# A two-layer attention and gMLP kernel: the spatial bias loaded once and whole, two weights loaded later, a P ring of 41 places and a new scheduler table

## The chip, the cores and the metric

The kernel runs on one core of one Trainium2 chip. The metric is device time in microseconds, the median of several runs. A core has TensorE (PE, matrix products into PSUM), VectorE (DVE), ScalarE (ACT, here the exponentials and GELUs), GpSimd (POOL) and SyncE (SP, which here issues every DMA). Each engine works through its own list of instructions in order; between engines semaphores say what is finished.

## The reference

Four blocks follow each other on an input of 2048 rows by 512, in bfloat16: attention, gated MLP, and both once more with the same weights. Each block normalises its input and adds its result to it.

```python
def _A_ref(x, wq, wk, wv, wo):
    H = 32; Dh = D // H                        # 32 heads of 16, one shared key and value head
    q = (x @ wq).reshape(B, S, H, Dh).transpose(0, 2, 1, 3)
    k = x @ wk
    v = x @ wv
    p = _softmax(einsum('bhqd,bkd->bhqk', q, k) * Dh ** (-0.5))
    o = einsum('bhqk,bkd->bhqd', p, v)
    return o.transpose(0, 2, 1, 3).reshape(B, S, H * Dh) @ wo

def _B_ref(x, w_in, w_sp, b_sp, w_out):
    z = _gelu(einsum('bsd,df->bsf', x, w_in))  # F = 1792, halves of 896
    z1 = z[..., :Fh]
    z2 = _layernorm(z[..., Fh:])
    g = einsum('ts,bsf->btf', w_sp, z2) + b_sp[None, :, None]
    return einsum('bsf,fd->bsd', z1 * g, w_out)

x = A_x
x = x + _A_ref(_layernorm(x), ...)
x = x + _B_ref(_layernorm(x), ...)
x = x + _A_ref(_layernorm(x), ...)
x = x + _B_ref(_layernorm(x), ...)
```

The product with `w_sp` is the spatial sum: it mixes all 2048 rows, and `b_sp` is its bias, one value for each of the 2048 output rows `t`.

## The kernel before

**A planner writes the program.** The kernel is Python that plans the whole execution before it emits it. Every piece of work is a `Task` with an engine, a cost and predecessors; `Sched` walks through planned time, and at every event each idle engine picks what is ready by priority (`step_act`, `step_dve`, `step_pool`, `step_pe`, `step_sp`). The order in which tasks are picked is the order of instructions on the engine; on the chip each waits for its semaphores, not for planned times. What the planner takes wrongly, for instance the landing of a DMA, becomes a wait on the chip, and everything behind it on that engine waits too. The preferences of the planner (how many scores DVE gets, how deep products with V go, when other work is let in) are class attributes of `Kernel`; the table `PLAN` sets other values for steps of 1250 ns of planned time (`follow`, `STEP`).

**Attention.** Rows are normalised tile by tile (16 tiles of 128 rows): `ln` writes `xn`, a DMA transposes it into `z1`'s space (lines 1634, `z<-xn`; the first two tiles go through PE, L1773), PE makes keys and values (L1871, L1874) and queries (L1901). A score matmul (L2468) covers 128 keys and 512 query columns of a head, into one of eight PSUM banks. Two engines turn scores into unnormalised probabilities P: ACT by an exponential, one bank at a time (L2665) or two (L2666), and DVE by an integer form (L2557) whose two further terms, the ramps, are made on POOL or DVE (L2561, L2577, one, two or four at a time). A block on ACT takes one place of the ring `Pb`, a block on DVE three. `NPS` is the number of places, of 1 KB in each partition; a place is free again when the product with V (L2725) has read it. `slot_ok` and `pick_exp` let an exponential or ramp be planned only when a place is free.

The queries come in chunks (`CHUNKS`). When a chunk is finished, `attn_out` copies the sums out (`oT`, L1959), transposes them by DMA into `oP`, divides (reciprocal L2105, product L2122 on POOL), transposes again (`onT`), multiplies by `wo` (L2065), adds to `X`, normalises and transposes into `xnT2`. The last chunk of a layer goes through PE instead of DMA.

**MLP.** `mlp_in` multiplies by `w_in` (L2161, L2222) and applies GELU on ACT in bursts between exponentials, ten in all, each with two loads of ACT's function table (L2968). `spatial` adds up the spatial sum in five passes over the source rows, in each layer; a pass takes the rows whose `z2` is ready, runs beside attention, and goes through four quarters of 512 output rows (`tc`). For each quarter `slab` loads the transposed part of `w_sp` into `wstr` (L1642, eight places of one tile, so two quarters), and for each of seven blocks `f` PE sums (L2280) and DVE adds the result to `gp` (L2290). In the first pass the addend is the bias, in later ones `gp` itself. The last pass (`last_pass`: L2319, L2321, DVE L2329, POOL L2340) gates with `z1` and multiplies by `w_out` (L2350).

**The bias.** `bspc` holds one quarter, 512 values, copied to all partitions. For every quarter of the first pass SP loads it anew, 128 KB as written, after the last addition of the previous quarter has read it (`bs_use`):

```python
if pi == 0:
    lb = self.dma(self.bspc[:], self.B_b_sp[tc * 512:(tc + 1) * 512].partition_broadcast(P), 131072,
                  self.bs_use, prio=2, tag="ldb", gate=lambda: self.s.t > self.WSP_FROM)
```

**Loads of weights.** `x`, `wk`, `wv` and `wq` are issued at the start. `wo` (512 KB), `w_in` (1792 KB) and `w_out` (896 KB) have a gate: they may be planned when planned time has passed `W_FROM` = 45000 ns. Loads for the spatial sum have the gate `WSP_FROM` = 75000 ns. All DMAs, transpositions included, go through SP's one queue. `dma_w` is the planner's cost of a `wstr` load on SP.

The functions that follow are those that the change touches and what calls them.

Of the kernel before, what the change touches and what calls it, by code (L numbers as in the profile page):

```python
# [6 lines left out]
BF16 = mybir.dt.bfloat16  # L7
# [63 lines left out]
def c_mm(n, cols):  # L71
# [5 lines left out]
    9: dict(FILL_MIN=3, PV_EFF=0.8, ACT_MAX=1, DVE_HIGH=1200),  # L77
    10: dict(PV_MAX=3, PV_LEAST=4),
    11: dict(ACT_LOW=700, FILL_BUSY=3, PV_LEAST=4, DVE_LEAD=-300),
    12: dict(ACT_LOW=1050, FILL_BUSY=3, PV_LEAST=4, DVE_LEAD=300),  # L80
    13: dict(ACT_LOW=1050, FILL_BUSY=3, PV_LEAST=4, DVE_LEAD=300, POOL_TOP=2500),
    15: dict(SLACK_HI=650, POOL_TOP=2500),
    16: dict(PV_LEAST=4),
    17: dict(PV_LEAST=4),
    18: dict(PV_LEAST=4, SHARE=0.45),
    19: dict(PV_MAX=4, DVE_LEAD=300, DVE_HIGH=1200, QUADP=0),
    20: dict(SLACK_HI=800, FILL_MIN=4, PV_MAX=4, DVE_LEAD=300, POOL_TOP=2500, QUADP=0),
    21: dict(SLACK=350, PV_EFF=0.8),
    22: dict(SLACK=350, PV_LEAST=4, PV_EFF=0.8),
    23: dict(SLACK=350, ACT_LOW=700, PV_LEAST=4, PV_EFF=0.8, COLS=0),  # L90
    24: dict(SLACK=350, ACT_LOW=1400, PV_LEAST=4, PV_EFF=0.8, COLS=0),
    25: dict(SLACK=200, DVE_LEAD=-300, POOL_TOP=2500, SCORE_CAP=5),
    26: dict(SLACK=200, DVE_LEAD=-300, POOL_TOP=3500, SCORE_CAP=5),
    27: dict(SLACK=200, DVE_LEAD=-300, POOL_TOP=3500, SCORE_CAP=5),
    28: dict(SLACK=200, DVE_LEAD=-300, POOL_TOP=3500, MISC_T=700, ACT_MAX=1, SCORE_CAP=5),
    29: dict(SLACK=200, DVE_LEAD=-300, MISC_T=700, ACT_MAX=1, SCORE_CAP=5),
    30: dict(SHARE=0.31, POOL_TOP=2500),
    31: dict(SHARE=0.45, POOL_TOP=2500, QUADP=0),
    32: dict(FILL_MIN=4, PV_EFF=0.8),
    33: dict(PV_LEAST=4, QUADP=0),  # L100
    34: dict(PV_LEAST=4, QUADP=0),
    35: dict(PV_LEAST=4, SHARE=0.4, MISC_T=2500, QUADP=0),
    36: dict(ACT_LOW=1700, PV_LEAST=4, PV_EFF=0.8, SHARE=0.4, MISC_T=2500, DVE_HIGH=2400, QUADP=0),
    37: dict(ACT_LOW=1700, PV_LEAST=4, PV_EFF=0.8, SHARE=0.4, POOL_TOP=2500, MISC_T=2500, DVE_HIGH=2400, QUADP=0),
    38: dict(ACT_LOW=1700, PV_LEAST=4, PV_EFF=0.8, SHARE=0.4, POOL_TOP=2500, MISC_T=2500, SCORE_CAP=5, DVE_HIGH=2400, QUADP=0),
    39: dict(ACT_LOW=1700, PV_LEAST=4, PV_EFF=0.8, SHARE=0.45, POOL_TOP=2500, MISC_T=2500, SCORE_CAP=5, DVE_HIGH=2400, QUADP=0, QUADD=0),
    40: dict(PV_LEAST=8, SHARE=0.31, SCORE_CAP=7, DVE_HIGH=1200),
    42: dict(PV_LEAST=4),
    43: dict(SLACK_HI=300, PV_EFF=0.8, MISC_T=700, DVE_HIGH=1200),
    44: dict(SLACK_HI=300, PV_EFF=0.8, MISC_T=700, DVE_HIGH=1200),  # L110
    45: dict(SLACK_HI=300, PV_EFF=0.8, MISC_T=700, DVE_HIGH=1200),
    46: dict(SLACK_HI=300, PV_EFF=0.8, POOL_TOP=2500, MISC_T=2500, DVE_HIGH=2400),
    47: dict(POOL_TOP=2500),
    48: dict(POOL_TOP=2500),
    49: dict(FILL_BUSY=3, DVE_LEAD=-300, HOLD=400),
    51: dict(FILL_BUSY=3, SHARE=0.28, POOL_TOP=3500, HOLD=400),
    52: dict(FILL_BUSY=3, SHARE=0.28, POOL_TOP=3500, HOLD=400, ACT_MAX=1),
    53: dict(POOL_TOP=7000),
    54: dict(POOL_TOP=7000),
    55: dict(SLACK=450, SLACK_HI=400, PV_LEAST=8, POOL_TOP=3500, SCORE_CAP=7),  # L120
    56: dict(SLACK=450, SLACK_HI=400, PV_LEAST=8, POOL_TOP=3500, SCORE_CAP=7),
    57: dict(SLACK=450, SLACK_HI=400, PV_LEAST=8, POOL_TOP=3500, SCORE_CAP=7),
    58: dict(SLACK=450, SLACK_HI=400, ACT_LOW=1400, PV_LEAST=8, POOL_TOP=3500, SCORE_CAP=7, QUADD=0),
    59: dict(SLACK=450, SLACK_HI=650, ACT_LOW=1400, PV_MAX=1, PV_LEAST=8, POOL_TOP=3500, SCORE_CAP=7, QUADD=0),
    60: dict(SLACK=450, SLACK_HI=650, ACT_LOW=1400, FILL_BUSY=3, PV_MAX=1, PV_LEAST=8, POOL_TOP=3500, SCORE_CAP=7, DVE_HIGH=1200, QUADD=0),
    61: dict(SLACK=450, SLACK_HI=650, ACT_LOW=1400, FILL_BUSY=3, PV_MAX=1, PV_LEAST=8, POOL_TOP=3500, SCORE_CAP=7, DVE_HIGH=1200, QUADD=0),
    63: dict(ACT_MAX=1),
    64: dict(ACT_LOW=900, PV_MAX=4, SHARE=0.28, HOLD=0, MISC_T=700),
    65: dict(MISC_T=2500, COLS=0),
    66: dict(COLS=0),  # L130
# [12 lines left out]
    81: dict(PV_MAX=4, DVE_LEAD=-600, POOL_TOP=7000, COLS=0),
    82: dict(PV_MAX=1),
    83: dict(FILL_MIN=3, POOL_TOP=2500, MISC_T=2500),
    84: dict(SLACK=350, ACT_LOW=1700, FILL_MIN=3, PV_MAX=3, MISC_T=2500, DVE_HIGH=1200),
    85: dict(ACT_LOW=1050, SHARE=0.36),
    86: dict(ACT_LOW=1050, PV_EFF=0.8, SHARE=0.36, HOLD=400),
    87: dict(SHARE=0.31),
    88: dict(FILL_BUSY=3, SHARE=0.28, DVE_LEAD=300, POOL_TOP=3500),  # L150
    89: dict(SHARE=0.36),
    90: dict(SHARE=0.36, POOL_TOP=2500),
    91: dict(SHARE=0.36, POOL_TOP=2500, MISC_T=2500),
    92: dict(FILL_BUSY=4, PV_MAX=4, SHARE=0.36, POOL_TOP=2500, MISC_T=2500),
    93: dict(FILL_BUSY=4, PV_MAX=4, SHARE=0.36, POOL_TOP=2500, MISC_T=2500),
    94: dict(FILL_BUSY=4, PV_MAX=4, SHARE=0.36, POOL_TOP=2500, MISC_T=2500),
    96: dict(FILL_MIN=3, SHARE=0.28, POOL_TOP=2500, MISC_T=2500),
    97: dict(SLACK=150, FILL_MIN=3, SHARE=0.28, POOL_TOP=2500, MISC_T=2500, SCORE_CAP=7),
    99: dict(SCORE_CAP=5),
    100: dict(PV_LEAST=4, SCORE_CAP=5),  # L160
    102: dict(POOL_TOP=2500),
    104: dict(PV_LEAST=4),
    105: dict(SHARE=0.4, HOLD=400),
    106: dict(ACT_LOW=1050, SHARE=0.4, POOL_TOP=2500, HOLD=400, DVE_HIGH=2400),
    107: dict(SLACK_HI=300, PV_MAX=4, PV_EFF=0.8),
    108: dict(SLACK_HI=300, PV_MAX=4, PV_EFF=0.8, POOL_TOP=2500),
    109: dict(SLACK_HI=300, PV_MAX=4, PV_EFF=0.8, POOL_TOP=2500, SCORE_CAP=5),
    110: dict(SLACK=600, SLACK_HI=650, FILL_MIN=3, SHARE=0.45),
    111: dict(SLACK=450, SLACK_HI=650, FILL_MIN=3, SHARE=0.45, QUADP=0),
    112: dict(SLACK=350, SLACK_HI=650, FILL_MIN=3, SHARE=0.45, COLS=3300, QUADP=0),  # L170
    113: dict(SLACK=350, SLACK_HI=650, FILL_MIN=3, SHARE=0.45, POOL_TOP=7000, COLS=3300, QUADP=0),
    114: dict(SLACK=350, SLACK_HI=650, FILL_MIN=3, PV_LEAST=4, SHARE=0.45, POOL_TOP=7000, COLS=3300, QUADP=0),
    115: dict(SLACK=350, SLACK_HI=650, FILL_MIN=3, PV_LEAST=4, SHARE=0.45, POOL_TOP=7000, COLS=3300, QUADP=0),
    116: dict(SLACK=350, SLACK_HI=650, ACT_LOW=1400, FILL_MIN=3, PV_LEAST=4, SHARE=0.45, POOL_TOP=7000, COLS=3300, DVE_HIGH=1200, QUADP=0),
    117: dict(SLACK_HI=800, FILL_MIN=3, POOL_TOP=3500, SCORE_CAP=7),
    118: dict(SLACK_HI=800, FILL_MIN=3, DVE_LEAD=300, POOL_TOP=3500, SCORE_CAP=7),
    119: dict(SLACK_HI=800, FILL_MIN=3, DVE_LEAD=300, POOL_TOP=3500, ACT_MAX=1, SCORE_CAP=7),
    121: dict(SLACK_HI=800, POOL_TOP=3500),
# [2990 lines left out]
```

## Time and profile before

| What | Before |
|---|---|
| median of three runs | 1503.27 us (1502.33 to 1505.92) |
| profiled execution, its own time | 1499.42 us |
| its span, first to last instruction | 1497.7 us |
| PE busy | 1433.2 us (96%) |
| DVE busy | 1383.0 us (92%) |
| ACT busy | 1377.4 us (92%) |
| POOL busy | 1037.3 us (69%) |
| mean granted clock of PE | 0.998 |
| bytes moved by DMA | 47.55 MB |
| exponentials of two banks, of one | 1212, 339 |

The profile is of one execution, and its times are from the first instruction. The page gives each engine's busy time; the chain of work that ended last, followed back from the end; and groups of equal instructions with their number, busy time, mean, and the idle time of the engine just before them with what ended it. A mean is from issue to end: where instructions overlap, their distance is shorter. The trace can be asked besides for waits by who waited for whom, for engines' busy time in stretches, and for the chain or the instructions in order of time. A line number names the line of the kernel that recorded the instruction.

In outline: the first attention layer runs from about 10 to 690 us, with GELU bursts and the first four passes of the spatial sum in it; the seam to the second layer takes until about 800, the second layer until 1435, and the rest is the tail.

### The profile page before, as it was taken

The numbers are of one execution on the slowest core, as the hardware profiler recorded it, in microseconds if no ns is written. First come the engines' busy times: TensorE is split into PE (matmuls) and PEld (weight loads), VectorE is DVE, ScalarE is ACT, GpSimd is POOL, SyncE is SP. The second block draws the span as 40 slices with busy tenths as digits, with TensorE's granted clock in tenths as the row PEclk, the third lists the DMA queues.
The fourth block names the chain that finished last, engine by engine and source line by source line (L and its number), as shares of the span: only waits on it lengthen the run. The fifth ranks groups of instructions, "written<-read, shape, count | busy, mean of one in ns | idle before, by whom it ended". The sixth has DMA issues, their size and how long they took to land.

```text
span 1497.7 us, 35502 instructions
## 1 busy us (share of the span) xinstructions
PE 1433.2 (96%) x14120; PEld 473.1 (32%) x14120; DVE 1383.0 (92%) x2605; ACT 1377.4 (92%) x1725; POOL 1037.3 (69%) x1152
## 2 busy tenths in 40 slices
PE   8999899999999999999999988999999999999999
PEld 3332232222322322233643322322223223222345
DVE  8899998999899999989767999899998999999886
ACT  7999999999999999996589999999999999999950
POOL 6677768878688688864114767677776786888737
PEclk9999999999999999999999999999999999999999
DMA  4420001112011111112121001001111111211111
GB/s 111 114 43 12 9 18 26 26 26 40 18 26 33 23 32 30 37 20 40 21 41 32 16 12 16 15 23 26 26 37 19 30 33 19 44 30 28 28 33 57
DMA packets 156627, 47.55 MB, mean 32 GB/s; under 512 B 148913, under 2 KB 155953, under 8 KB 156465
## 3 DMA queue, kind: packets, MB, share of 16 engines
q1 hardware_dynamic: 156464, 45.28, 15.2%
q8 instruction: 115, 1.88, 0.5%
q14 instruction: 48, 0.39, 0.1%
HBM read 6.98 MB, written 2.10 MB: 6 GB/s over the span
## 4 chain that ended last, share of the span: by engine, by line
ACT 53%; PE 36%; DVE 7%; DMA 2%; issue 0%; POOL 0%; SPq 0%; DVEq 0%
ACT Pb L2666 46%; PE ps_all L2725 9%; PE ps_all L2468 9%; PE ps_all L2280 7%; ACT Pb L2665 6%; DVE Pb L2557 4%; PE ps_all L2161 3%; PE ps_all L2350 3%; PE ps_all L2222 3%; PE ps_all L2321 1%; DMA bspc<-in_B_b_sp_dram 1%; DVE Pb L2577 1%; DMA z<-xn 1%; DVE gp L2290 1%; ACT L2968 1%
## 5 line engine op out<-in xcount | busy, mean ns | idle before, releaser
L2666 ACT ACTIVATE Pb<-ps_all 128x1024 bf16<-128x1024 f32 x1212 | 1154.3, 1138 | 12.8 <-PE ps_all L2468 11.9
L2577 POOL TENSOR_SCALAR Pb<-Pb 128x1024 int16<-128x1024 int16 (+1 forms) x732 | 803.4, 1097 | 212.0 <-DVE Pb L2577 163.4
L2557 DVE TENSOR_SCALAR Pb<-ps_all 128x512 int16<-128x512 f32 x1333 | 858.2, 684 | 39.7 <-PE ps_all L2468 33.6
L2468 PE MATMUL ps_all<-z,kT 32*128 32x512 bf16 x4096 | 535.8, 385 | 45.3 <-ACT Pb L2666 25.4
L2725 PE MATMUL ps_all<-Pb,V 128*32 128x512 bf16 x6762 | 531.9, 385 | 4.2 <-DVE Pb L2557 1.0
L2468 PEld LDWEIGHTS ps_all<-z,kT 32*128 32x128 bf16 x4096 | 136.2, 91 | 570.6 <-ACT Pb L2666 393.5
L2280 PE MATMUL ps_all<-wstr,z 128*128 128x512 bf16 x784 | 224.1, 384 | 1.8 <-DVE gp L2290 1.4
L2665 ACT ACTIVATE Pb<-ps_all 128x512 bf16<-128x512 f32 x339 | 205.8, 719 | 6.1 <-PE ps_all L2468 5.9
L2577 DVE TENSOR_SCALAR Pb<-Pb 128x1024 int16<-128x1024 int16 (+1 forms) x451 | 195.7, 471 | 0.4
L2725 PEld LDWEIGHTS ps_all<-Pb,V 128*32 128x32 bf16 x6762 | 124.6, 94 | 225.9 <-issue 119.5
L2290 DVE TENSOR_TENSOR gp<-ps_all,gp 128x512 f16<-128x512 f32 x168 | 113.2, 683 | 1.2 <-PE ps_all L2280 0.8
L2280 PEld LDWEIGHTS ps_all<-wstr,z 128*128 128x128 bf16 x784 | 51.5, 97 | 93.8 <-issue 41.7
L1724 POOL TENSOR_SCALAR ln_rs<-ln_mv 128x1 f32<-128x1 f32 (+2 forms) x52 | 11.6, 225 | 97.2 <-DVE ln_mv L1734 90.4
L2561 POOL TENSOR_SCALAR Pb<-Pb 128x512 int16<-128x512 int16 x79 | 48.8, 617 | 40.3 <-DVE Pb L2577 22.3
L2350 PE MATMUL ps_all<-w_out,z 128*128 128x512 bf16 x224 | 58.4, 380 | 0.3 <-DVE z L2329 0.2
L2122 POOL TENSOR_TENSOR o_norm<-oP,rdn 128x128 bf16<-128x128 bf16 (+1 forms) x84 | 39.7, 495 | 21.4 <-DVE Pb L2577 12.1
L2161 PE MATMUL ps_all<-w_in,xnT 128*128 128x448 bf16 x256 | 53.2, 353 | 0.9 <-ACT xnT L1785 0.7
L2222 PE MATMUL ps_all<-xnT,w_in 128*128 128x512 bf16 (+3 forms) x336 | 51.5, 308 | 0.0
L2174 DVE BATCH_NORM_STATS2 st<-z 128x6 f32<-128x448 bf16 x64 | 35.6, 604 | 13.8 <-ACT z L2166 13.6
L1959 DVE CAST oT<-ps_all 128x512 bf16<-128x512 f32 x64 | 43.9, 686 | 4.2 <-PE ps_all L2725 4.1
L1733 DVE BATCH_NORM_STATS2 ln_st<-X 128x6 f32<-128x512 bf16 x64 | 43.3, 682 | 1.7 <-DMA X<-in_A_x_dram 1.5
L2236 ACT ACTIVATE z<-ps_all 128x512 bf16<-128x512 f32 (+2 forms) x62 | 31.4, 562 | 13.7 <-PE ps_all L2222 13.6
(76 smaller groups left out, 768.4 us busy)
## 6 DMA issues: line engine op xcount, KB each, us to landing
out_dram<-X SPq DMA_DIRECT2D x16, 128.0 KB, 1.7
w_in<-in_B_w_in_dram SPq DMA_DIRECT2D x1, 1792.0 KB, 9.1
X<-in_A_x_dram SPq DMA_DIRECT2D x3, 512.0 KB, 7.8
bspc<-in_B_b_sp_dram SPq DMA_DIRECT2D x8, 128.0 KB, 3.7
oP<-oT SPq DMA_TRANSPOSE x60, 2.4
w_out<-in_B_w_out_dram SPq DMA_DIRECT2D x1, 896.0 KB, 7.2
wstr<-in_B_w_sp_dram SPq DMA_TRANSPOSE x40, 4.1
X<-in_A_x_dram SPq DMA_DIRECT2D x2, 256.0 KB, 3.2
```

The costliest lines, as they stand in the source:

```text
L2161: ins = e.matmul(self.ps32[:, b, 0:448], self.xnT2[:, buf, kd, o:o + P], self.w_in[:, kd, FH + h * 448:FH + (h + 1) * 448], start=(kd == 0 ...
L2222: ins = e.matmul(self.ps32[:, b, i * nq:(i + 1) * nq], self.w_in[:, kd, f * P:(f + 1) * P], self.xnT2[:, buf, kd, x0:x0 + nq], start=(kd = ...
L2280: ins = e.matmul(self.ps32[:, b, :], self.z2[:, (s0 + i) % Z2R, f * P:(f + 1) * P], self.wstr[:, sl[i // SLAB][1] + i % SLAB, :], start=(i ...
L2290: return Task("dve", c_ps(512), lambda e: e.tensor_tensor(self.gp[:, tc, f, :], self.ps32[:, bank(), :], src, ALU.add), dps, self.GP_P, ta ...
L2350: ins = e.matmul(self.ps32[:, b, :], self.z1[:, tc, f, o:o + P], self.w_out[:, f, :], start=(f == 0), stop=(f == NF - 1))
L2468: ins = e.matmul(self.ps32[:, jb[i].i, :], self.kT[32 * j:32 * j + 32, u.half, kt * P:(kt + 1) * P], q, tile_position=(32 * j, 0), start=T ...
L2557: return lambda e: e.tensor_scalar(self.Pi[:, dst(), :], self.ps32[:, bank, :], EBIAS + lo, lo, op0=ALU.add, op1=ALU.max)
L2561: return lambda e: e.tensor_scalar(self.Pi[:, dst(), :], self.Pi[:, src(), :], lo, 1.0, op0=ALU.add, op1=ALU.mult)
L2577: return lambda e: e.tensor_scalar(self.several(self.Pi, dst), self.several(self.Pi, src), lo, 1.0, op0=ALU.add, op1=ALU.mult)
L2665: return e.activation(self.Pb[:, ss[0], :], self.ps32[:, bs[0], :], ACTF.Exp, scale=ESCALE)
L2666: return e.activation(self.two(self.Pb, *ss), self.two(self.ps32, *bs), ACTF.Exp, scale=ESCALE)
L2725: ins = e.matmul(self.ps32[32 * j:32 * j + 32, u.bank.i, :], self.V[:, var, kt, :], self.Pb[:, sl.i, :], tile_position=(0, 32 * j), start= ...
```

## The change

- `bspc` grows from 512 to 2048 values in each partition, and one DMA (`ldbs`, 512 KB as written) fills it for both layers, with the gate `WSP_FROM`. The eight loads by quarter and `bs_use` go. The first pass reads its quarter out of it.
- `w_in` and `w_out` get the gate `WSP_FROM` (75000) instead of `W_FROM`. Their priorities put them behind the `wstr` loads and the bias. `wo` keeps `W_FROM`, which goes from 45000 to 48000.
- `NPS` goes from 44 to 41. Three places are 3 KB in each partition, as much as `bspc` grows.
- `dma_w` gives SP's cost of a `wstr` load by another formula: 2010 ns for four tiles (1859 before), 1410 for three (1645), 1230 for two (1430). It changes the plan only.
- `PLAN` is another table: 1071 steps have an entry instead of 1051, 952 have one in both, and none of these is the same. The order on every engine is therefore another. Line numbers rise by about 20 (L2665 and L2666 become 2686 and 2687, L2725 becomes 2746, L2290 becomes 2313).

```diff
 PLAN = {
-    9: dict(FILL_MIN=3, PV_EFF=0.8, ACT_MAX=1, DVE_HIGH=1200),
-    10: dict(PV_MAX=3, PV_LEAST=4),
...
 }
...
     WSP_FROM = 75000
-    W_FROM = 45000
-    NPS = 44
+    W_FROM = 48000
+    NPS = 41
...
-        self.bspc = self.sb([P, 512], BF16, "bspc")
+        self.bspc = self.sb([P, S], BF16, "bspc")
...
         def cost():
-            occ = 1000 + nbytes / 610.0
+            occ = 1230 + 600 * max(0.0, nbytes / 131072 - 2.7)
             self.wide_done = max(self.s.t + 3200, self.wide_done) + 500 + nbytes / 250.0
...
         self.ldo = self.dma(self.wo[:], ..., 524288, prio=2.5, gate=late)
-        self.ldin = self.dma(self.w_in[:], ..., 1835008, prio=2.5, gate=late)
-        self.ldout = self.dma(self.w_out[:], ..., 917504, prio=2.5, gate=late)
+        def later():
+            return s.t > self.WSP_FROM
+        self.ldin = self.dma(self.w_in[:], ..., 1835008, prio=2.5, tag="ldb", gate=later)
+        self.ldout = self.dma(self.w_out[:], ..., 917504, prio=2.6, tag="ldb", gate=later)
+        self.ldbs = self.dma(self.bspc[:], self.B_b_sp.partition_broadcast(P), 524288, prio=2.4, tag="ldb", gate=later)
...
                 if pi == 0:
-                    lb = self.dma(self.bspc[:], self.B_b_sp[tc * 512:(tc + 1) * 512].partition_broadcast(P), 131072,
-                                  self.bs_use, prio=2, tag="ldb", gate=lambda: self.s.t > self.WSP_FROM)
-                    self.bs_use = []
+                    lb = self.ldbs
...
-                        src = self.bspc[:] if pi == 0 else self.gp[:, tc, f, :]
+                        src = self.bspc[:, tc * 512:(tc + 1) * 512] if pi == 0 else self.gp[:, tc, f, :]
...
-                    if pi == 0:
-                        self.bs_use.append(outs[0])
...
-        self.bs_use = []
```

More of the change, by code (lines that the diff above doesn't have):

```diff
@@ L87 @@
[L87 to L94, printed above, removed]
@@ new lines @@
+    67: dict(FILL_BUSY=3, PV_MAX=3, PV_LEAST=8),
+    68: dict(PV_MAX=1, HOLD=0),
+    69: dict(HOLD=400),
+    70: dict(SLACK_HI=800, COLS=0),
+    71: dict(SLACK_HI=800, POOL_TOP=3500, COLS=0),
+    72: dict(SLACK=350, SCORE_CAP=5),
+    73: dict(SLACK=350, FILL_BUSY=3, POOL_TOP=7000, HOLD=400, SCORE_CAP=5, QUADD=0),
+    74: dict(COLS=0),
+    75: dict(PV_MAX=1, QUADD=0),
+    77: dict(ACT_LOW=700),
+    78: dict(ACT_LOW=700),
+    79: dict(ACT_LOW=700),
+    80: dict(ACT_LOW=1050, FILL_MIN=3, PV_MAX=1, HOLD=400, MISC_T=700, QUADP=0),
@@ new lines @@
+    350: dict(FILL_BUSY=3, PV_MAX=1, PV_LEAST=8, HOLD=400, COLS=3300),
+    351: dict(POOL_TOP=7000, MISC_T=700),
+    352: dict(POOL_TOP=7000, MISC_T=700),
+    354: dict(POOL_TOP=2500),
+    355: dict(PV_MAX=1),
+    356: dict(PV_MAX=1),
+    357: dict(SHARE=0.28, POOL_TOP=2500),
+    358: dict(SLACK=450, ACT_LOW=500),
+    359: dict(ACT_MAX=1),
+    360: dict(FILL_BUSY=3, COLS=0),
+    361: dict(SLACK_HI=800, PV_MAX=1, POOL_TOP=7000, SCORE_CAP=5, DVE_HIGH=2400),
+    362: dict(SHARE=0.31, DVE_HIGH=1200),
@@ new lines @@
+    553: dict(SLACK=600, HOLD=400, COLS=3300, DVE_HIGH=2400),
+    554: dict(SLACK=600, HOLD=400, COLS=3300, DVE_HIGH=2400),
+    555: dict(ACT_LOW=1050, SCORE_CAP=7),
+    556: dict(SHARE=0.36),
+    557: dict(DVE_LEAD=300),
+    558: dict(FILL_MIN=3, DVE_LEAD=300),
+    562: dict(QUADD=0),
+    563: dict(ACT_MAX=1, QUADP=0),
+    564: dict(ACT_MAX=1, QUADP=0),
+    565: dict(ACT_MAX=1, QUADP=0),
+    566: dict(ACT_MAX=1, QUADP=0),
+    567: dict(ACT_MAX=1, QUADP=0),
+    568: dict(ACT_MAX=1),
@@ new lines @@
+    736: dict(SLACK=450, HOLD=0),
+    737: dict(SLACK=450, HOLD=0),
+    739: dict(PV_LEAST=4, DVE_LEAD=300, MISC_T=700),
+    740: dict(PV_LEAST=4, DVE_LEAD=300, HOLD=400, MISC_T=700),
+    741: dict(FILL_MIN=4),
+    742: dict(POOL_TOP=2500),
+    743: dict(PV_MAX=1),
+    744: dict(ACT_LOW=900, MISC_T=2500, COLS=2900),
+    745: dict(DVE_HIGH=1200),
+    746: dict(ACT_LOW=900, SCORE_CAP=7),
+    747: dict(COLS=0),
+    748: dict(COLS=0),
+    749: dict(PV_EFF=0.8),
+    750: dict(PV_EFF=0.8, SHARE=0.45, DVE_LEAD=-300),
@@ new lines @@
+    815: dict(PV_LEAST=8, SHARE=0.36, MISC_T=700, DVE_HIGH=1200),
+    816: dict(SLACK_HI=400, FILL_BUSY=3, SHARE=0.24),
+    817: dict(SLACK_HI=400, FILL_BUSY=3, PV_MAX=1, SHARE=0.24),
+    818: dict(POOL_TOP=2500),
+    819: dict(POOL_TOP=2500),
+    820: dict(PV_EFF=0.8, HOLD=400),
+    821: dict(SLACK=600, PV_MAX=1, POOL_TOP=7000, MISC_T=700, QUADP=0),
+    822: dict(HOLD=400, QUADP=0),
+    824: dict(PV_MAX=1),
+    825: dict(PV_MAX=4),
+    826: dict(PV_MAX=4, PV_EFF=0.8, COLS=3300),
+    827: dict(FILL_MIN=4, PV_MAX=4),
@@ L1128 @@
+    1181: dict(SLACK=200, SLACK_HI=400, FILL_MIN=4, PV_MAX=1, SHARE=0.28, DVE_LEAD=300, QUADP=0, QUADD=0),
+    1184: dict(SLACK=600, FILL_BUSY=3, PV_LEAST=4),
+    1185: dict(SLACK=600, FILL_BUSY=3, PV_LEAST=4),
+    1186: dict(SLACK=600, FILL_BUSY=3, PV_LEAST=4),
+    1189: dict(SLACK=450, SLACK_HI=400, QUADP=0),
+    1190: dict(SLACK=450, SLACK_HI=400, QUADP=0),
 }
@@ L1816, in setup @@
         self.ldo = self.dma(self.wo[:], self.A_wo.rearrange("(c p) n -> p c n", p=P), 524288, prio=2.5, gate=late)
-        self.ldin = self.dma(self.w_in[:], self.B_w_in.rearrange("(kd p) f -> p kd f", p=P), 1835008, prio=2.5, gate=late)
-        self.ldout = self.dma(self.w_out[:], self.B_w_out.rearrange("(c p) n -> p c n", p=P), 917504, prio=2.5, gate=late)
+        def later():
+            return s.t > self.WSP_FROM
+        self.ldin = self.dma(self.w_in[:], self.B_w_in.rearrange("(kd p) f -> p kd f", p=P), 1835008, prio=2.5, tag="ldb", gate=later)
+        self.ldout = self.dma(self.w_out[:], self.B_w_out.rearrange("(c p) n -> p c n", p=P), 917504, prio=2.6, tag="ldb", gate=later)
+        self.ldbs = self.dma(self.bspc[:], self.B_b_sp.partition_broadcast(P), 524288, prio=2.4, tag="ldb", gate=later)
         self.ldv = ldv
```

2042 lines of the change are left out of this document (1001 added, 1041 removed).

## The prediction

> **What bounds the kernel now.** I read the page first: its engine shares, the clock row, the chain and the costliest groups.
>
> ```profile
> PE 1433.2 (96%) x14120; PEld 473.1 (32%) x14120; DVE 1383.0 (92%) x2605; ACT 1377.4 (92%) x1725; POOL 1037.3 (69%) x1152
> ...
> ACT 53%; PE 36%; DVE 7%; DMA 2%; issue 0%; POOL 0%; SPq 0%; DVEq 0%
> ...
> L2666 ACT ACTIVATE Pb<-ps_all 128x1024 bf16<-128x1024 f32 x1212 | 1154.3, 1138 | 12.8 <-PE ps_all L2468 11.9
> ...
> L2665 ACT ACTIVATE Pb<-ps_all 128x512 bf16<-128x512 f32 x339 | 205.8, 719 | 6.1 <-PE ps_all L2468 5.9
> ```
>
> ACT's exponentials (L2665, L2666) carry half of the chain. They idle only 12.8 + 6.1 = 18.9 us before them, nearly all for a score matmul (L2468). Outside the seam between the layers and the tail, ACT is full: whoever delays a score matmul by more than the scores in stock moves the end. So I looked for that idle time, in a table of stretches (columns: stretch; length, then busy us of PE, PEld, DVE, ACT, POOL; clock; DMA share; GB/s):
>
> ```profile
> 256.00:264.00 8.00, 6.76 (x73) 1.67 (x70) 6.54 (x12) 6.95 (x9) 5.03 (x6) 1.00 0.60 85
> 320.00:324.00 4.00, 3.02 (x36) 0.68 (x28) 3.35 (x6) 3.50 (x5) 3.68 (x5) 1.00 0.02 7
> 1000.00:1008.00 8.00, 6.50 (x46) 1.35 (x42) 5.87 (x10) 5.71 (x7) 5.11 (x5) 0.79 0.02 5
> 1060.00:1064.00 4.00, 2.52 (x21) 0.56 (x21) 2.74 (x5) 2.75 (x4) 2.47 (x4) 1.00 0.06 15
> 50.00:54.00 4.00, 1.92 (x24) 0.71 (x21) 1.97 (x6) 2.21 (x4) 2.09 (x2) 1.00 1.21 226
> 54.00:60.00 6.00, 5.86 (x56) 1.21 (x56) 4.31 (x10) 4.88 (x6) 2.23 (x4) 0.72 0.08 25
> ```
>
> In the first four ACT lacks 1.05 + 0.50 + 2.29 + 1.25 = 5.1 us, in the last two 1.79 + 1.12 = 2.9. The waits and the chain in order of time name the causes:
>
> ```profile
> DVE gp L2290 <- DMA bspc<-in_B_b_sp_dram: 5.6, 4, 1.8
> ```
> ```profile
> 46.61 5.77 DMA z<-xn
> 52.38 0.14 issue
> 52.52 0.38 PE ps_all L1871 x4
> ```
> ```profile
> w_in<-in_B_w_in_dram SPq DMA_DIRECT2D x1, 1792.0 KB, 9.1
> ```
>
> Four times the addition to `gp` stands at the head of DVE for the next quarter of the bias; the scores that DVE turns into P (L2557) queue behind it, their PSUM banks stay taken, PE can issue no scores, ACT dries up. Four other quarters of the bias cost ACT nothing. At 46.61 the last transposition of `xn` takes 5.77 us (median of its group 2.5) because `w_in`, issued at 42.75, takes 9.1 us to land; PE waits 1.93 us for it at L1871.
>
> **Part by part, in us of the profiled execution** (span 1497.7, own time 1499.42; the median of the runs, 1503.27, lies 3.85 above and I let that stand).
>
> *Bias whole.* Eight SP issues of 0.58 us and 128 KB become one of 512 KB, at about 77. First use is the first pass of the spatial sum at 229: 150 us of cover. L2290 then never waits for the bias: -5.1. Next late could be `wstr` of the same quarter, but it is asked for two quarters ahead (issued at 254.99, needed from about 285, median 4.1 to land), and the first pass otherwise waits only for PE, 0.3 in all now. Bounds: 0 if another wait stands in the same place, -5.1; I take -5.1, since the DMA is named as ender of all four.
>
> *w_in, w_out later.* In the instruction lists of the new program all 14 transpositions of `xn` are issued before `wo`, and `w_in`, `w_out` come behind two `wstr` loads, at about 78. The last transposition should take 2.5, no wait: -2.9. `wo` (4.7 to land) goes out about 48, first read at 77.9. What is delayed instead: 3.2 MB at the 400 GB/s of the stretch from 46 to 50 are 8 us, behind two `wstr` loads, so the queue is free at some 88 to 90. The next SP entries in the old order are a transposition for `oP` at 86.09, one for `xnT` at 87.42, one for `oP` at 104.21. The first two may land 3.3 late (5.77 - 2.5); but the reciprocal that reads `oP` waits for the half issued at 104.21 and runs at 108.61, and `xnT` is read at 213.5. Cost 0; without that cover up to 3.3.
>
> *P ring 44 to 41, new table.* No step of the table is equal in both, so engines are compared by counts. ACT: pairs 1212 to 1190, singles 339 to 385. Back to back a pair takes 0.917 (18 in 16.50 in the chain), a single 0.49 (5 in 2.46): 46 x 0.49 - 22 x 0.917 = +2.4, on the bound engine, so all of it counts. DVE: 2 scores fewer, 3 double ramps fewer, 1 quadruple and 10 single ramps more: by the means of the rows -1.4 - 1.3 + 0.7 + 4.2 = +2.2 at most; beside ACT, taken 0, kept for the range. POOL: 25 double ramps more, 15 quadruple and 2 single fewer: 26.1 - 28.5 - 1.2 = -3.6; POOL idles 460, nothing. PE: 4 products with V and 16 warming matmuls fewer, nothing.
> The ring itself has no row: no wait of ACT ends at a product with V (L2725), which frees places. 6762 places are taken in about 1330 us of attention, 5.1 per us, so 41 hold 8.0 us of work where 44 hold 8.6. Bounds: 0, and the idle before the exponentials that is left after the two repairs, 18.9 - 8.0 = 10.9, doubled. A new order can also halve it (-5.5). I take 0, because no present wait is for a place.
>
> *Tail.* Behind the last score PE has 45 matmuls of the spatial sum instead of 57, nine of them taken out between the last L2065 and the transposition of `xn` at 1449.14. There 24 take 5.18; `xn` is done at 1448.22, so PE is 0.9 late: -0.9 (bounds 0 and 12 x 0.216 = -2.6). The four additions and 12 matmuls that move forward find DVE idle 3.2 us in 1375 to 1400 beside the gelu burst; without it +2.4. The seam holds the same matmuls but for 3 products with V.
>
> *SP cost of `wstr`* (planner alone): the rows give 1.2 to 2.8 for an issue, SP idles most of the time: 0.
>
> Sum: -5.1 - 2.9 + 2.4 - 0.9 = -6.5. Span 1491.2, own time 1492.9, median 1496.8.
>
> **A rule weighed.** The clock row shows 0.50 from 55 to 58 and from 1004 to 1006, after gaps on PE of 1.93 and 1.41 us; after 1.19 (261.74) and 1.48 (1062.01) it stays 1.00. 2.1 of the 8.0 us of ACT's idleness fall under the low clock (1.12 in 54 to 60, 0.96 in 1004 to 1008). The Trainium skill ("TensorE: Matmul & The Clock Gate", Part 1) says that the clock falls after at least one idle window of about 3.4 us, and that the window runs free of the program. No gap here is that long: by the rule the drops are not these gaps' doing and would stay; by the rows they follow two of the gaps, and go.
>
> **Rivals.**
> 1. *The drops stay.* If the low clock comes from something else than the two gaps, its 2.1 remain: -4.4, median 1498.9. For it: a gap of 1.48 without a drop. Against: the clock is 1.00 everywhere else.
> 2. *The order gives it back.* A new order meets new late events that no plan shows; with half of the remaining idle more (+5.5): -1.0, 1502.3. For it: everything moves; 46 more singles show that pairs are harder to get. Against: the known late ends, both DMAs, are gone.
> 3. *The ring stops ACT (slower).* Whenever products with V lag by more than 8.0 us, ACT halts for a place until PE catches up, 3 / 5.1 = 0.59 a time. The likely place is the spatial sum, where PE and DVE have the most besides: 32 quarters in the passes before the last. Once in each: +18.9, sum +12.4, 1515.7. It decides from 6.5 / 0.59 = 11 halts on, and passes 0.3% at 19. For it: DVE full (24.7 of 25 in 1075 to 1100). Against: the waits of ACT, none for a place.
> 4. *More goes.* The new order also halves the remaining idle: -12.0, 1491.3.
> That the change does nothing is excluded: the bias load is once in the new list.
>
> **How the numbers follow.** Forecast 0.48 (own range 1493 to 1500), rival 1 0.06, rival 2 0.22, rival 3 0.12, rival 4 0.12. 0.3% is 4.5 us, about what a measurement of this kernel can tell from no change: the forecast lies beyond that in about 0.42 of its 0.48, rival 1 half, rival 4 wholly: faster 0.57; rival 3 slower, with 0.01 from rival 2: 0.13; same 0.30. The range runs from beyond rival 4 (-5.5 and the tail's -2.6 together: 1489.6, and 2.6 for what the runs differ) to 1508: rival 3 with 19 halts, or the forecast with the late transposition's 3.3, DVE's 2.2, the tail's 2.4 and 3.3 of new idle.
>
> **What would show it.** Right: no wait of the addition to `gp` for the bias; ACT full from 50 to 60 with the clock at 1.00; last `xn` transposition 2.5; 1190 and 385 exponentials with some 11 us idle before them; 63 us from the last score to the end (63.6 now). Wrong: idle before the exponentials above 18, or ended by products with V or by a DMA; `oP`'s reciprocal waiting at about 90; a clock drop in a new place.

## The result and the profile after

| | Before | After |
|---|---|---|
| median of the runs | 1503.32 us (1502.33 to 1505.92) | 1487.32 us (1486.33 to 1488.82) |
| profiled execution, its own time | 1499.42 us | 1488.82 us |
| its span | 1497.7 us | 1487.1 us |
| ACT busy, and idle in the span | 1377.4, 120.3 us | 1377.5, 109.6 us |
| mean granted clock of PE | 0.998 | 0.999 |

The changed kernel takes 0.9892 of the time (95% interval 0.9875 to 0.9909), 16.0 us less. The forecast was 6.5 less. By the sums of the prediction its range began at 1487.0, so this time lies at the very edge of it, and outside the forecast's own 1493 to 1500. The profiled executions differ by 10.6 us only, and that gap between the two comparisons turns out to be more than half of the error.

The page of the changed kernel, its engine shares, chain and exponentials:

```profile
PE 1427.5 (96%) x14100; PEld 469.7 (32%) x14100; DVE 1382.2 (93%) x2611; ACT 1377.5 (93%) x1749; POOL 1036.8 (70%) x1160
...
ACT 65%; PE 29%; DVE 3%; DMA 2%; issue 1%; POOL 1%; POOLq 0%
...
L2687 ACT ACTIVATE Pb<-ps_all 128x1024 bf16<-128x1024 f32 x1190 | 1130.1, 1155 | 7.4 <-PE ps_all L2489 6.9
...
L2686 ACT ACTIVATE Pb<-ps_all 128x512 bf16<-128x512 f32 x385 | 226.6, 720 | 3.4 <-PE ps_all L2489 3.3
```

ACT carries 65% of the chain instead of 53%. Its idle time before exponentials is 7.4 + 3.4 = 10.8 us instead of 18.9, and nearly all of that still ends at a score matmul (now L2489).

The six stretches that the prediction showed, in the changed kernel (length, then busy us of PE, PEld, DVE, ACT, POOL; clock; DMA share; GB/s):

```profile
50.00:54.00 4.00, 3.71 (x47) 0.93 (x39) 3.88 (x9) 4.00 (x6) 2.05 (x3) 1.00 0.00 0
54.00:60.00 6.00, 5.87 (x73) 2.16 (x70) 6.00 (x14) 6.00 (x8) 3.78 (x7) 1.00 0.15 25
...
256.00:264.00 8.00, 8.00 (x79) 2.00 (x76) 7.81 (x16) 8.00 (x10) 5.65 (x5) 1.00 0.29 66
...
320.00:324.00 4.00, 4.00 (x38) 1.04 (x39) 4.00 (x8) 4.00 (x5) 2.81 (x4) 1.00 0.01 2
...
1000.00:1008.00 8.00, 7.95 (x77) 1.94 (x74) 8.00 (x16) 8.00 (x11) 6.45 (x7) 1.00 0.09 18
...
1060.00:1064.00 4.00, 4.00 (x48) 1.07 (x47) 4.00 (x8) 4.00 (x6) 3.28 (x4) 1.00 0.00 0
```

ACT is full in all six, and the clock is 1.00 in all six, where it was 0.72 and 0.79 in two of them. The additions to `gp` (first pass L2313, last pass L2350) and the reciprocal that reads `oP` wait as follows, in the waits of DVE (who waits for whom: us in total, times, longest):

```profile
DVE gp L2350 <- PE ps_all L2342: 1.8, 3, 1.2
...
DVE gp L2313 <- PE ps_all L2303: 0.5, 1, 0.5
...
DVE rdn L2130 <- DMA oP<-oT: 0.2, 1, 0.2
```

No wait for the bias is left. The reciprocal's 0.2 us lie in the second layer, between 900 and 1300 us; from 70 to 120 us, behind `w_in` and `w_out`, it does not wait for a transposition at all.

Where the 10.6 us between the two profiled executions lie is read from ACT, in the last one as in the first: its busy time is the same (+0.1), so all is idle time. Before exponentials it is -8.1. The rest is mostly the wait for the rows that go through PE (`xnT` and `z`, L1785, now L1805). ACT's waits of the kernel before:

```profile
ACT xnT L1785 <- PE ps_all L1773: 24.4, 2, 12.4
ACT z L1785 <- PE ps_all L1773: 17.8, 4, 9.2
```

and of the changed kernel:

```profile
ACT xnT L1805 <- PE ps_all L1793: 22.6, 2, 11.3
ACT z L1805 <- PE ps_all L1793: 17.3, 4, 9.2
```

That is 42.2 to 39.9, -2.3: of `xnT`'s two waits the one at the seam is 0.8 shorter (12.1 to 11.3) and the one in the tail 1.2 (12.4 to 11.2). GELUs wait 0.8 less (18.1 to 17.3), everything else on ACT 0.5 more: -8.1 - 2.3 - 0.8 + 0.5 + 0.1 = -10.6.

### The profile page after: what moved, and what is told of

Read it like the earlier page. It is cut to its first block, busy times and chain, and to the rows that moved or that the text cites. A ratio compares the mean times of both kernels' runs of the same rounds, so it can differ in the third digit from the quotient of the medians.

```text
span 1487.1 us, 35548 instructions
## 1 busy us (share of the span) xinstructions
PE 1427.5 (96%) x14100; PEld 469.7 (32%) x14100; DVE 1382.2 (93%) x2611; ACT 1377.5 (93%) x1749; POOL 1036.8 (70%) x1160
## 4 chain that ended last, share of the span: by engine, by line
ACT 65%; PE 29%; DVE 3%; DMA 2%; issue 1%; POOL 1%; POOLq 0%
ACT Pb L2687 56%; ACT Pb L2686 7%; PE ps_all L2489 7%; PE ps_all L2746 7%; PE ps_all L2303 5%; PE ps_all L2371 3%; PE ps_all L2186 3%; PE ps_all L2247 2%; DMA z<-xn 2%; PE ps_all L2342 1%; ACT L2989 1%; DVE Pb L2578 1%; DVE gp L2313 1%; ACT z L2261 1%; DVE st L2199 0%
## 5 line engine op out<-in xcount | busy, mean ns | idle before, releaser
L2687 ACT ACTIVATE Pb<-ps_all 128x1024 bf16<-128x1024 f32 x1190 | 1130.1, 1155 | 7.4 <-PE ps_all L2489 6.9
L2489 PE MATMUL ps_all<-z,kT 32*128 32x512 bf16 x4096 | 532.1, 384 | 39.3 <-ACT Pb L2687 23.8
L2489 PEld LDWEIGHTS ps_all<-z,kT 32*128 32x128 bf16 x4096 | 134.9, 90 | 566.4 <-ACT Pb L2687 391.1
L2686 ACT ACTIVATE Pb<-ps_all 128x512 bf16<-128x512 f32 x385 | 226.6, 720 | 3.4 <-PE ps_all L2489 3.3
L2313 DVE TENSOR_TENSOR gp<-ps_all,gp 128x512 f16<-128x512 f32 x168 | 113.1, 680 | 0.9 <-PE ps_all L2303 0.5
```

The lines of the kernel that those rows point to most:

```text
L2313: return Task("dve", c_ps(512), lambda e: e.tensor_tensor(self.gp[:, tc, f, :], self.ps32[:, bank(), :], src, ALU.add), dps, self.GP_P, ta ...
L2489: ins = e.matmul(self.ps32[:, jb[i].i, :], self.kT[32 * j:32 * j + 32, u.half, kt * P:(kt + 1) * P], q, tile_position=(32 * j, 0), start=T ...
L2686: return e.activation(self.Pb[:, ss[0], :], self.ps32[:, bs[0], :], ACTF.Exp, scale=ESCALE)
L2687: return e.activation(self.two(self.Pb, *ss), self.two(self.ps32, *bs), ACTF.Exp, scale=ESCALE)
```

## The experiments

**The theory after the result:** the two repairs (bias whole, weights late) give nearly all of the gain, and more in the runs than in one profile, because each stall that goes takes a chance of a low clock with it. **The rivals:** the new order gives the rest; or the gain of the repairs is what one execution showed, and the median of before was high for another reason.

**1. The kernel before once more.** No edit.

> The kernel before once more, unchanged. Theory 1 (the two late DMAs cost more in an ordinary run than in the one profiled): its runs spread over several us, about 1499 to 1506, and this profile, another execution, shows other lost time of ACT at the same places (261, 321, 1001, 1061 and 50 to 60 us) than 8.0 us in all. Theory 2 (the new order and table brought what I had not counted): the lost time at these places is again 8 us within 1, and the runs lie where they did, 1503.

Measured: 1500.79 us (1498.03 to 1508.15), ratio 0.9997 (0.9977 to 1.0017). Stretches of this second profile of the same program:

```profile
54.00:60.00 6.00, 5.97 (x53) 1.11 (x49) 3.74 (x9) 4.52 (x5) 1.86 (x3) 0.62 0.00 0
...
1000.00:1008.00 8.00, 7.49 (x76) 1.85 (x69) 7.77 (x14) 7.81 (x10) 6.22 (x7) 1.00 0.01 2
...
1060.00:1064.00 4.00, 3.04 (x23) 0.69 (x27) 3.29 (x6) 2.15 (x3) 2.24 (x2) 0.76 0.00 0
```

At 1000 to 1008 ACT lacks 0.19 us instead of 2.29, and the clock is 1.00; at 1060 to 1064 it lacks 1.85 instead of 1.25, under a clock of 0.76; at 54 to 60 it is 1.48 instead of 1.12, under 0.62. The sum over ten stretches around the eight quarters of the bias and the start is nearly the same (8.1 and 8.0), its place is not. The stalls belong to the program; which quarter is late, and whether the clock drops behind it, belongs to the execution.

The runs show what the drops cost. Over 65 runs of the kernel before, in this and the later comparisons, a straight line through time against mean granted clock rises by 1.07 us for each 0.001 of clock, from 1496.8 at 1.000; the runs lie from 1496.9 (0.998) to 1509.7 (0.989), and the mean clock is 0.995. By that line the drops cost this kernel 5.3 us on average, and 2.1 in the profile that I had priced (0.998). The line does not say behind which stall a drop stood.

**2. The bias whole, nothing else.** The order of every engine is kept as it was; the ring keeps 44 places. The whole bias lies where the sum of the last block `f` will be written, which is free until then. Nothing is left out; the seven other planned loads remain on SP as loads of 4 KB, for which nobody waits, and one more load fetches the bias for the second layer.

```diff
+self.gpb = self.gp[:].bitcast(BF16)
...
+if n8 == 0:
+    lb.fn = lambda e: e.dma_start(self.gpb[:, :, NF - 1, :], self.B_b_sp.partition_broadcast(P).rearrange("p (c n) -> p c n", c=4))
+else:
+    lb.fn = lambda e, n8=n8: e.dma_start(self.bspc[:, n8 * 16:n8 * 16 + 16], self.B_b_sp[0:16].partition_broadcast(P))
...
-src = self.bspc[:] if pi == 0 else self.gp[:, tc, f, :]
+src = self.gpb[:, tc, NF - 1, :] if pi == 0 else self.gp[:, tc, f, :]
...
+sp.insert(onT[0], (list(waits.items()), lambda e: e.dma_start(dst, src), key, self.lbs[0]))
```

> Every engine's order as in the kernel before. Only the bias is another: loaded whole, once for each layer, into the part of gp that is written last in each quarter, so that P keeps 44 places; where the plan had the other loads, 4 KB go to a place nobody reads. Priced from the trace: -5.1 us. Theory 1: more than that in the median, -7 to -10. Theory 2: -4 to -6.

Measured: 1494.36 us (1492.82 to 1498.27), ratio 0.9954 (0.9935 to 0.9973): -6.6. No wait of DVE for the bias is left, and the stall at 50 to 60 stays, with a clock of 0.50 in 54 to 60. The repair is worth the 5.1 of the forecast, or somewhat more.

**3. The weights late, nothing else.** The order of every engine but SP is kept; SP issues `w_in` and `w_out` after the second load of `wstr`.

```diff
+mine = [x for x in sp if x[3] is self.ldin or x[3] is self.ldout]
+rest = [x for x in sp if not (x[3] is self.ldin or x[3] is self.ldout)]
+at = [i for i, x in enumerate(rest) if x[3].tag == "ldw"][1] + 1
+self.s.prog["sp"] = rest[:at] + mine + rest[at:]
```

> Every engine's order as in the kernel before, but SP issues w_in and w_out behind the second load of wstr. Priced from the trace: -2.9 us, the last transposition of xn takes 2.5 us, the clock stays at 1.00 from 50 to 60. Theory 1: -4 to -6 in the median. Theory 2: -2 to -4. If the two loads now hold up what comes behind them: 0 or slower.

Measured: 1496.24 us (1494.31 to 1503.61), ratio 0.9961 (0.9941 to 0.998): -4.7, where the forecast had 2.9. The profiled execution is one of the slower ones (1500.63, mean clock 0.993), and it shows something new, a clock of 0.50 from about 17 to 37 us. The stretch with most of it:

```profile
25.00:50.00 25.00, 23.96 (x236) 8.07 (x235) 18.86 (x50) 21.16 (x28) 14.07 (x25) 0.75 0.29 39
```

Its 64th score matmul comes 6.9 us later than in experiment 1's profile, which has none of that. Just before the clock falls, PE has waited 0.94 us before it makes keys and values (L1871, at 16.14), at a place that this edit does not touch. ACT is full from 50 to 60 all the same: the stall is gone.

**4. Both repairs on the old order.**

```diff
 def edit(self):
+    self.move_weights()
+    self.whole_bias()
```

> Both edits on the order of the kernel before: the change without its ring, its table and its planner cost. Priced from the trace: -8.0 us. Theory 1: -12 to -15, so nearly all of the measured -16. Theory 2: -7 to -9, so that ring, table and order are worth -7 to -9 more.

Measured: 1490.03 us (1489.82 to 1490.38), ratio 0.9917 (0.989 to 0.9943): -10.9, about the sum of the two alone (6.6 + 4.7). Two of its stretches, and then three of ACT's waits:

```profile
54.00:60.00 6.00, 5.64 (x69) 2.14 (x62) 5.48 (x10) 6.00 (x10) 4.19 (x8) 1.00 0.12 25
...
1000.00:1008.00 8.00, 7.84 (x92) 2.09 (x89) 8.00 (x16) 8.00 (x10) 5.75 (x6) 1.00 0.08 16
```
```profile
ACT xnT L1790 <- PE ps_all L1778: 24.4, 2, 12.4
...
ACT Pb L2679 <- PE ps_all L2481: 7.3, 10, 1.4
...
ACT Pb L2678 <- PE ps_all L2481: 3.1, 6, 0.8
```

ACT is full in all ten stretches (62.00 of 62.00 us). The waits for scores, 7.3 + 3.1, are those of the changed kernel (6.9 + 3.3). The two spans differ by 1.5 us (1488.6 and 1487.1), and of all the waits only that for `xnT` differs by as much: 24.4 here, as in the kernel before, and 22.6 in the changed one. The six runs lie within 0.6 us, all at a mean clock of 0.999 or 1.000, where the 27 of before beside them lie within 12.7. The drops behind the two stalls are gone. One is left in this profile, behind no wait of PE longer than 0.5 us:

```profile
1120.00:1125.00 5.00, 4.21 (x30) 0.95 (x30) 4.37 (x8) 5.00 (x8) 4.67 (x5) 0.72 0.60 76
```

Six runs do not show that the longer drops are gone for good: the one near the start in experiment 3 comes back on this order in experiment 8.

**5. The changed kernel once more.** No edit; it ran on another chip, beside experiments 6 to 8.

> The changed kernel once more, beside the kernel before on the same chip, to set against the two repairs on the old order (1490.0, ratio 0.9917). Theory 2 (the new order and table brought what I had not counted): 1484 or less, so that the order is worth 6 or more. Theory 1 (nearly all of it is the two DMAs): 1486 to 1489, the order worth 1 to 4.

Measured: 1488.55 us (1487.01 to 1489.97), ratio 0.9913 (0.9899 to 0.9927), 13.0 us less than before on that chip. So part of the 16.0 of the first comparison is which executions were drawn. The ratio of experiment 4 lies in this interval: by the medians, ring, table and order beyond the two repairs are worth some 1.5 us, which these runs cannot tell from nothing. The runs at a mean clock of 1.000 hint at more: 1486.3 to 1487.0 for the changed kernel, 1489.8 to 1490.1 for experiment 4, though on different chips. Six of the nine runs of the changed kernel are at 0.999 and lie higher, 1487.9 to 1490.0; its two profiles each have one drop of the clock, at 789 and at 1440 us.

**6. The weights early again, in the changed kernel.** Its order is kept; SP issues `w_in` before the last transposition of `xn` and `w_out` after it, about as the kernel before did.

```diff
+i = [i for i, x in enumerate(rest) if x[3].tag == "TA"][13]
+self.s.prog["sp"] = rest[:i] + win + rest[i:i + 1] + wout + rest[i + 1:]
```

> The order of the changed kernel on every engine, but SP issues w_in ahead of the last transposition of xn and w_out right behind it, as before the change. Theory 1: +4 to +5 us against the changed kernel, as the opposite edit took 4.7 from the old order, with a wait of PE for that transposition and a clock drop behind it, and wider spread. Theory 2: +2 to +3.

Measured: 1495.72 us (1494.7 to 1497.06), ratio 0.9961 (0.9947 to 0.9975): 7.2 above the changed kernel. A piece of the chain in order of time (start, length), and the stretch behind it:

```profile
42.85 7.68 DMA z<-xn
```
```profile
54.00:60.00 6.00, 6.00 (x53) 1.34 (x55) 4.18 (x8) 4.52 (x6) 1.37 (x2) 0.60 0.02 6
```

The transposition takes 7.68 us behind `w_in` (the group's median is 2.5). PE waits up to 3.5 us for it, and the clock behind it is 0.60. In 50 to 60 ACT lacks 2.42 + 1.48 us, and from 25 to 50 it is busy 1.56 us less than in the changed kernel. PE's wait is longer than the 1.93 us of the kernel before, so this is more than the old stall put back.

**7. The bias by quarters again, in the changed kernel.** Quarters 1 to 3 of each layer are loaded once more, each after the last addition of the quarter before, and the first addition waits for the load.

```diff
+sp.insert(i, ([(prev.key, prev.val)], lambda e, tc=tc: e.dma_start(
+    self.bspc[:, tc * 512:(tc + 1) * 512], self.B_b_sp[tc * 512:(tc + 1) * 512].partition_broadcast(P)), key, sp[i - 1][3]))
...
+dve[at] = (list(w) + [(key, 16)], fn, k, t)
```

> The order of the changed kernel on every engine, but SP loads the second to fourth quarter of the bias anew in each layer's first pass, each after the last addition of the quarter before, and the addition waits for it. P keeps 41 places. Theory 1: +5 to +7 us against the changed kernel, as the opposite edit took 6.6 from the old order. If the new order had more in stock at these places: +3 or less.

Measured: 1496.43 us (1494.33 to 1501.69), ratio 0.997 (0.9958 to 0.9982): 7.9 above the changed kernel. The wait of DVE, and two stretches:

```profile
DVE gp L2314 <- DMA bspc<-in_B_b_sp_dram: 6.6, 5, 2.2
```
```profile
256.00:264.00 8.00, 5.70 (x58) 1.53 (x62) 5.82 (x11) 6.27 (x7) 4.68 (x5) 1.00 0.34 82
...
1060.00:1064.00 4.00, 2.83 (x28) 0.90 (x33) 3.83 (x8) 2.96 (x4) 1.63 (x2) 1.00 0.00 0
```

The five waits are at the quarters that wait in experiment 1's profile, on another order; the one at 1000 us is only 0.2 here, and ACT stays full there. In the medians the bias is worth 6.6 us on the old order and 7.9 on the new one.

**8. Pairs split.** The forecast charged 2.4 us for 22 pairs fewer and 46 singles more; ACT's busy time did not rise. Here 45 pairs of experiment 4's kernel become 90 singles, at the same places of the same order.

```diff
+if n == 2 and pair % 27 == 5:
+    e.activation(self.Pb[:, ss[0], :], self.ps32[:, bs[0], :], ACTF.Exp, scale=ESCALE)
+    return e.activation(self.Pb[:, ss[1], :], self.ps32[:, bs[1], :], ACTF.Exp, scale=ESCALE)
```

> Both repairs on the order of the kernel before, and 45 of the 1212 exponentials of two banks, evenly spread, are made as two of one bank each. By the rows, 2 x 0.49 - 0.917 = 0.063 us each: 1490.0 + 2.8 = 1492.8, if ACT is the bound wherever they lie. This is the term of +2.4 for the singles of the new order. If other engines leave ACT that much slack: 1490 to 1491.

Measured: 1495.73 us (1491.52 to 1499.26), ratio 0.9956 (0.9937 to 0.9975). The median says +5.7 over experiment 4, which ran on another chip, but it is mostly not the exponentials. The profiled execution (1497.29, clock 0.995) in stretches of 5 us:

```profile
15.00:20.00 5.00, 3.88 (x40) 1.65 (x38) 4.20 (x12) 4.43 (x8) 3.09 (x7) 0.80 0.14 26
20.00:25.00 5.00, 5.00 (x40) 0.99 (x38) 3.51 (x10) 3.79 (x5) 2.24 (x6) 0.50 0.37 73
25.00:30.00 5.00, 5.00 (x43) 1.89 (x39) 3.62 (x10) 4.03 (x5) 3.00 (x6) 0.50 0.05 10
```

A low clock from about 18 to 31 us, behind a wait of PE of 0.97 us, costs 4.5 us between the first and the 64th score matmul; four of the eight runs have a mean clock of 0.993 to 0.995. From the 128th to the last score matmul it takes 1371.2 us, against 1370.0 in experiment 4: +1.2. The two runs at a mean clock of 1.000 (1491.52 and 1491.63) lie 1.7 above those of experiment 4 at 1.000 (1489.82 to 1490.06). My price for these 45 was 45 x (0.98 - 0.917) = 2.8; they cost 1.2 to 1.7, though ACT's busy time rises by 3.7 (1376.1 to 1379.8). A split pair on ACT is not wholly on the path. Whether the low clock in the first 50 us is made likelier by the splits, these runs don't say: experiment 3 has it too, without them.

**9 to 11. The ring alone, the new table alone, the old table on the changed kernel.** Here the planner makes its plan anew, so that the order on every engine moves, as it did in the change itself. The first differs from the kernel before in one line:

```diff
-    NPS = 44
+    NPS = 41
```

> The kernel before with 41 places in the ring instead of 44 and nothing else; the planner makes its plan anew with the old table, and once it differs anywhere, every later choice falls elsewhere. Theory (a table fits one plan only: an entry belongs to a moment of planned time, and with another plan behind it the work that it was chosen for is no longer there): 5 to 25 us slower than before's 1501, the time lost in many small idle stretches of ACT, waiting for score matmuls; no wait of ACT ends at a product with V (L2725). Rival 1 (the ring stops ACT, rival 3 of the prediction): slower as well, but with waits of ACT ended by products with V. Rival 2 (the table's values are good for any plan, and three places are nothing): within 3 us of before.

The second is the kernel before with the table of the changed one, and nothing else:

```diff
 PLAN = {
-    9: dict(FILL_MIN=3, PV_EFF=0.8, ACT_MAX=1, DVE_HIGH=1200),
...
+    9: dict(SLACK=600, ACT_LOW=1400),
...
 }
```

> The kernel before with the new table and nothing else: bias by quarters, weights early, 44 places, old cost of a load of w_sp. Theory (a table fits one plan only): 5 to 25 us slower than before. Rival (the new table is the better one by itself): at most 1499, that is before's 1501 less the 1.5 us by which the changed kernel lies below the two repairs on the old order.

The third is the changed kernel with the table of before:

```diff
 PLAN = {
-    9: dict(SLACK=600, ACT_LOW=1400),
...
+    9: dict(FILL_MIN=3, PV_EFF=0.8, ACT_MAX=1, DVE_HIGH=1200),
...
 }
```

> The changed kernel with the table of before: bias whole, weights late, 41 places, new cost of a load of w_sp. Theory (a table fits one plan only): the two repairs are there (no wait for the bias, no late transposition), but the plan is a third one: 1495 to 1515, 6 to 26 above the changed kernel's 1488.6. Rival (the table hardly matters): 1490, as the two repairs on the old order.

Measured, beside before's 1502.19 on that chip:

| | time, us | ratio to before | exponentials, two banks / one | ACT busy | idle before exponentials |
|---|---|---|---|---|---|
| ring of 41 alone | 1583.46 | 1.0547 (1.0525 to 1.0568) | 861 / 1046 | 1418.4 | 52.4 |
| new table alone | 1574.64 | 1.0477 (1.0458 to 1.0497) | 856 / 1058 | 1418.9 | 46.7 |
| changed kernel, old table | 1567.97 | 1.0435 (1.0419 to 1.0451) | 896 / 974 | 1414.4 | 46.7 |

The exponentials with the ring of 41 alone, by the page:

```profile
L2666 ACT ACTIVATE Pb<-ps_all 128x1024 bf16<-128x1024 f32 x861 | 876.1, 1103 | 40.8 <-PE ps_all L2468 37.5
...
L2665 ACT ACTIVATE Pb<-ps_all 128x512 bf16<-128x512 f32 x1046 | 595.0, 700 | 11.6 <-PE ps_all L2468 10.7
```

And these are all the waits of ACT that end at a product with V (L2726 there) in the changed kernel with the old table:

```profile
ACT Pb L2667 <- PE ps_all L2726: 0.6, 1, 0.6
...
ACT Pb L2666 <- PE ps_all L2726: 0.3, 1, 0.3
```

The direction was expected, the size not: 66 to 81 us, where 5 to 26 had been. For the ring alone the span is 84.3 longer than before's: ACT is busy 41.0 more, since 351 pairs have become 707 singles, and idle 43.3 more. The three lose alike, with 41 places and with 44, with the bias by quarters and whole; so it is not ACT halting at a full ring, and its waits for a place are 0.9 us in one and none in the others. What they share is a plan and a table that were not made for each other: the scores come one at a time, and the pairs go. The rival "values good for any plan" falls, as does "the new table is the better one by itself".

What ring and table are worth in the change can therefore not be read from one of them alone. Together they give an order as good as the old one or a little better (experiments 4 and 5). Whether 44 places with a table searched for them would do better stays open; it needs a new search, which was not tried.

## Why the prediction was right and wrong

- *What bounds it, and the causes.* Right. Both late DMAs were on the path: taking each away on the old order gives 6.6 and 4.7, putting each back on the new order costs 7.9 and 7.2. In the profile of after, the idle before exponentials is 10.8 where "some 11" was forecast, -8.1 where -8.0 was.
- *The cover of what is delayed.* Right. The bias is issued at 72.85 us and the first addition waits for nothing but PE; behind `w_in` and `w_out` the reciprocal on `oP` loses nothing.
- *"The median of the runs, 1503.27, lies 3.85 above and I let that stand."* This is the step that failed most: it took the distance from the profiled execution to the median for an offset that the change leaves alone. In the changed kernel the median lies 1.50 below its profiled execution. The term thus changed by 3.85 + 1.50 = 5.35 us, of an error of 9.5. By the line of experiment 1, 3.2 of the 3.85 are the low clock that the average run of before met more of (0.995, 5.3 us) than the profiled one (0.998, 2.1 us). The profiled execution of the changed kernel met one drop that two of its four runs do not show. The rest is the draw: beside the later experiments before's median is 1500.9 to 1502.2, and in experiment 5 the change is worth 13.0. I had the two drops of one execution as 2.1 of the 8.0 and took them for all there was. How many of the other runs' drops stood behind the two stalls is not shown: the two profiles of before have drops nowhere else, but experiments 3 and 8 have one near the start, behind a wait that neither repair touches.
- *"+2.4, on the bound engine, so all of it counts."* Wrong: ACT is busy +0.1. The counts were right (1190 and 385). Experiment 4 has the exponentials of the kernel before and waits for scores about as often as the changed kernel (16 and 15 times); against it ACT is busy 1.4 us more (1376.1 to 1377.5), which is what the singles came to. The other 1.3 went the other way, and the sum had no term for it: from the kernel before to experiment 4 ACT's busy time falls from 1377.4 to 1376.1 with the same exponentials, while its waits for scores fall from 25 to 16. With the same exponentials again, experiment 3's profile has 31 waits and 1378.5. That each wait breaks the row, so that the last exponential before it runs to its end uncovered, would explain this; it is argued only. The split pairs too show the price as too high for the path, 1.2 to 1.7 for 2.8.
- *The tail, -0.9, and the seam, none.* From the last score matmul to the end 63.6 became 63.1, -0.5. ACT's wait for `xnT` is 1.2 shorter there and 0.8 at the seam, where I had said that the seam holds the same matmuls; why it is shorter there stays open. These and the GELU waits are -2.6 where the sum had -0.9. So the profiled executions add up: -6.5 forecast, -0.1 idle, -2.3 singles, -1.7 here, -10.6 measured. Parted by experiment 4's profile, the two repairs are -9.1 where -8.0 was forecast, and ring, table and order -1.5 where 2.4 - 0.9 = +1.5 was.
- *The ring, 0.* Right: ACT's waits name no product with V. But the argument looked for the ring on the chip, and its pressure and the table's act in the plan, where a wrong pairing costs 66 to 81 us. That none of it came is due to a table that fits its plan, which nothing in the profile of before could have told: here the forecast was lucky.
- *The rivals.* In the six stretches the drops did go with the gaps (1.00 in all), so rival 1 falls. But a drop in a new place, which the prediction names as a sign of being wrong, came at the seam (below). Rivals 2 and 3 did not happen (for rival 3 I had DVE at 24.7 of 25 us in 1075 to 1100; the row says 24.83, which changes nothing). Rival 4 forecast the nearest time (1491.3) for a reason that is wrong: the remaining idle before exponentials, 10.8, was not halved.

## What to carry to other kernels

Price a stall of PE by many runs, not by one profile: what it costs beside its own length is a chance of a lowered clock, and the spread of the runs with their mean clocks is where that shows. When a planned order is kept by its own table, test parts of a change on the old order by moving single instructions; a plan made anew with a table that was made for another one lost four to five per cent here, more than any repair in the change could bring. A small DMA that someone waits for must not stand behind a large one, and a buffer that can be reloaded only when its last reader is done is worth making larger, here for three places of a ring.

## What the runs showed of the hardware

The clock drops depend on the execution. In the changed kernel PE waits 1.31 us at 787.64 for a transposition of `xn`; behind it the first profile of this program shows, in a stretch of 5 us,

```profile
790.00:795.00 5.00, 5.00 (x54) 2.26 (x45) 1.89 (x3) 4.41 (x7) 0.06 (x1) 0.71 0.02 4
```

and the second, of experiment 5, in the same stretch:

```profile
790.00:795.00 5.00, 4.76 (x63) 2.29 (x53) 2.50 (x5) 5.00 (x7) 0.65 (x2) 1.00 0.13 26
```

The clock is once 0.71 and once 1.00. The drops have a common length. In the changed kernel the clock is 0.95 in 785 to 790 and 0.71 in 790 to 795: over 5 us each, 0.05 and 0.29 are missing, together 1.7 us of full clock, or 3.4 us at 0.50. The same working, from stretches of 5 us, gives 3.4 us for experiment 4's drop at 1120 us, 6.8 for the one at 50 us in experiment 1, 10.2 in experiment 2, 13.7 in experiment 8 and 20.5 in experiment 3: whole multiples of 3.4, within the rounding. So a stall can cost, beside its own length, one or more such pieces at half clock, and in other executions none.

Near the start, 0.50 was granted for 13 us or more in two executions (experiments 3 and 8), behind waits of PE of 0.94 and 0.97 us; in experiment 8's PE was busy 5.00 of 5.00 us meanwhile. Experiment 4, with the same order, has 1.00 there, and the two that had the low clock lost 6.6 and 4.5 us between the first and the 64th score matmul. The Trainium skill ("TensorE: Matmul & The Clock Gate", Part 1) says that the window in which idleness is judged runs free of the program; this dependence on the execution agrees with it. The same part of the Trainium skill says that the clock falls after at least one idle window of about 3.4 us; this does not fit the drops behind gaps of 1.41 and 1.93 us in the profile of before. Of the waits of PE shown here only the 3.5 us of experiment 6 is that long.
